# Logit weights of two token groups from one fp32 transpose, their products in fp32 on quarters of the array's columns

## The chip, the core and the metric

The kernel runs on one NeuronCore of one Trainium2 chip. The metric is the device time of one execution in microseconds; the median of three runs of the kernel before is 355.45 us (355.38 to 355.95). Engines are named as the profile names them: PE (TensorE's products; PEld its weight loads), DVE (VectorE), ACT (ScalarE), POOL (GpSimd), SP (SyncE, which issues the DMAs). PE's clock has two levels, 1.2 and 2.4 GHz; the profiled execution has a mean granted clock of 0.994, and 1.00 in every stretch that is read below.

## The reference, cut to what matters

```python
# attention: q, k, v are (2, 8, 576, 64); x becomes (1152, 512)
q_p, k_p = phi(q * scale), phi(k * scale)          # exp features, 128 of them
x = (q_p @ (k_p^T v)) / (q_p @ sum(k_p) + 1e-6)
# a dense layer, 512 -> 2048 -> 512
h = x @ w_in
g = h * (1 / (1 + exp(-1.702 * h)))
x2 = g @ w_out
# one expert per token
logits = x2 @ w_gate                                # (1152, 8)
expert_idx = argmax(logits, axis=1)
gate_w = softmax(logits)[expert_idx]
# tokens in order take the places of their expert until `capacity` (288) is full
out[i] = gate_w[i] * (relu(x2[i] @ w1[e]) @ w2[e])  # e = expert_idx[i]; 0 where no place was left
```

The dense layer's weights arrive as 64-bit floats and are decoded on the chip. w_in and w_out are cut along the 2048 into 16 chunks of 128 (m = 0 to 15).

## The kernel before

**Numbers.** Products that need fp32 accuracy are made of three fp32r products: a value is split into hi (rounded to fp32r) and lo (the rest), and mm3 (lines 81 to 84) adds hi*hi, hi*lo and lo*hi. Attention's own products and all transposes except those of w_out take plain fp32.

**Tokens.** The 1152 tokens form four groups G of GS = 288. Groups 0 and 2 go all the way: do_h makes h_ps for one chunk m (12 products of 128x288), gelu is taken twice by ACT (ghi in fp32r, line 544; g32 in fp32, line 545), DVE subtracts (glo, line 546), and do_y adds the chunk's share to four PSUM banks (12 more products). Of groups 1 and 3 only the logits are wanted at first; whether their tokens have a place left is found out later, and in these data no later branch runs. Their logits are taken without x2: with wp = w_out @ w_gate, a 2048 x 8 matrix, logits = g @ wp.

**Logit weights.** For each m, four steps on PE make 128 rows of wp: do_wt(m, 0) and do_wt(m, 1) transpose the chunk of w_out, hi and lo apart (four transposes each against identr, line 576; ACT copies each, line 577); do_wg multiplies them with w_gate (eight products of 128 columns, lines 585 and 587; ACT copies, line 589); do_wp transposes the 16x128 result back (line 594), and DVE reduces and splits it (lines 596 to 598). do_lg then adds g @ wp of one (G, m) to the bank lgt_ps with two products, ghi and glo (lines 610 and 613); groups 1 and 3 share the bank's 32 rows.

**Order.** The order of the work is a list of slots: seq has one do_h for each slot, by rounds. Round r has (0, r), (1, r - 3) and (3, r - 6) as far as they exist (L1 = 3, L3 = 6), 48 slots, then 16 slots of group 2. do_consume (do_y or do_lg) of a slot comes two slots later. slot(n, f) hangs other work on slot n: decoding, logit weights (do_wt at the slot of (1, m), the next steps half a slot apart), logits, choice of the experts, loads. A scheduler then places each engine's instructions, in about this order, and adds the waits; each engine runs its own list strictly in order.

**Decoding.** Each of the 32 chunks (in and out in turn) takes three DVE instructions, a, b and c (lines 220, 223, 226), through the int32 tile wf (two buffers) and back into every second word of the raw tile wraw; then d: ACT rounds hi (line 232) and POOL subtracts lo (line 233). Six chunks are decoded in the attention stage (P["dec"], steps 13 to 28), the other 26 from the dense layer's first slots on, 0.9 to 1 slot apart.

**Banks.** PSUM has eight banks: A (2: projections, h_ps), B and C (4: pj, then y), L and M. mbank alternates between L and M, and gives M alone while lgt_ps holds L.

Of the kernel before, what the change touches and what calls it, by code (L numbers as in the profile page):

```python
# [19 lines left out]
def linear_attention__moe__top1_moe_kernel(  # L20
# [106 lines left out]
    identr = const.tile([128, 128], F32R, name="identr")  # L127
    nc.vector.tensor_copy(identr, ident)
# [62 lines left out]
    w_raw = {}  # L191
# [19 lines left out]
    def decode(kind, m):  # L211
# [5 lines left out]
        f = gp.tile([128, DM], I32, tag="wf", name="wf", bufs=2)  # L217

# [240 lines left out]
    for s in range(NS + 1):  # L459
# [46 lines left out]
    wg_f = const.tile([128, KD, E], F32, name="wg_f")  # L506
    nc.sync.dma_start(out=wg_f, in_=moe2_w_gate.rearrange("(c p) e -> p c e", p=128))
    wg = const.tile([128, KD, 2, E], F32R, name="wg")
    nc.vector.tensor_copy(wg[:, :, 0], wg_f)
    nc.vector.tensor_tensor(wg[:, :, 1], wg_f, wg[:, :, 0].bitcast(F32), ALU.subtract)  # L510
# [7 lines left out]
    for r in range(NF + L3):  # L518
# [15 lines left out]
    def do_h(G, m):  # L534
# [32 lines left out]

    wts, wws = {}, {}

    def do_wt(m, i):  # L570
        src = w_out(m)[i]
        dst = gp.tile([128, DM], F32R, tag=f"wt{i}", name=f"wt{i}", bufs=1)
        ps = mbank("wt_ps")
        for c in range(KD):
            dc = slice(c * 128, c * 128 + 128)
            nc.tensor.transpose(ps[:, dc].bitcast(F32R), src[:, dc], identr)  # L576
        nc.scalar.copy(dst, ps)  # L577
        wts.setdefault(m, []).append(dst)

    def do_wg(m):  # L580
        th, tl = wts.pop(m)
        ps = mbank("wg_ps")
        for c in range(KD):
            dc = slice(c * 128, c * 128 + 128)
            nc.tensor.matmul(ps[:2 * E, :128], wg[:, c].rearrange("p a e -> p (a e)"), th[:, dc],
                             start=(c == 0), stop=False)
            nc.tensor.matmul(ps[:E, :128], wg[:, c, 0], tl[:, dc], start=False, stop=(c == KD - 1))
        t = gp.tile([2 * E, 128], F32, tag="wgt", name="wgt", bufs=1)
        nc.scalar.copy(t, ps[:2 * E, :128])
        wws[m] = t  # L590

    def do_wp(m):
        ps = mbank("wp_ps")
        nc.tensor.transpose(ps[:, :2 * E], wws.pop(m), ident[:2 * E, :2 * E])
        f = gp.tile([128, E], F32, tag="wpf", name="wpf", bufs=1)
        nc.vector.tensor_reduce(f, ps[:, :2 * E].rearrange("p (a e) -> p e a", a=2), AX, ALU.add)
        nc.vector.tensor_copy(wp[:, 2 * m + 1, 0], f)
        nc.vector.tensor_tensor(wp[:, 2 * m + 1, 1], f, wp[:, 2 * m + 1, 0].bitcast(F32), ALU.subtract)

    def do_lg(G, m):  # L600


        first = not held
        if first:
            held.append(bank("L", "lgt_ps"))
        g3 = G // 2
        ghi, glo = gs.pop((G, m))
        o = held[0]
        w = wp[:, 2 * m + 1 - g3:2 * m + 3 - g3].rearrange("p m a e -> p (m a e)")
        nc.tensor.matmul(o[:4 * E, :GS], w, ghi, start=first, stop=False)  # L610
# [3 lines left out]
        if last:  # L614
            nc.scalar.copy(lgt, held.pop()[:4 * E, :GS])
# [42 lines left out]
    def do_logits(G):  # L658
        if G % 2 == 0:
# [20 lines left out]
        nc.vector.tensor_reduce(  # L680
# [375 lines left out]
```

## Time and profile before

| | |
|---|---|
| median of three runs | 355.45 us (355.38 to 355.95) |
| the profiled execution | 356.26 us, of which its span (first to last instruction) is 354.4 us |
| PE busy | 332.9 us, 94% of the span, 2633 products |
| PEld busy | 318.0 us |
| DVE busy | 221.1 us |
| ACT busy | 189.2 us |
| POOL busy | 56.9 us |
| share of PE in the chain that ended last | 69%; DVE 13%, issue 6%, ACT 4%, DMA 4% |

In the profile a product's duration (0.30 us for 128x288) is longer than its time in the array, since products are pipelined and their ends are modelled. What a product costs PE is read from starts: the start of the next one less its own. Attention takes the first 100 us or so, the dense layer with its logits lasts until about 300 us, the experts' work follows; the stages overlap.

### The profile page before, as it was taken

The numbers are of one execution on the slowest core, as the hardware profiler recorded it, in microseconds if no ns is written. First come the engines' busy times: TensorE is split into PE (matmuls) and PEld (weight loads), VectorE is DVE, ScalarE is ACT, GpSimd is POOL, SyncE is SP. The second block draws the span as 40 slices with busy tenths as digits, with TensorE's granted clock in tenths as the row PEclk, the third lists the DMA queues.
The fourth block names the chain that finished last, engine by engine and source line by source line (L and its number), as shares of the span: only waits on it lengthen the run. The fifth ranks groups of instructions, "written<-read, shape, count | busy, mean of one in ns | idle before, by whom it ended". The sixth has DMA issues, their size and how long they took to land.

```text
span 354.4 us, 6927 instructions
## 1 busy us (share of the span) xinstructions
PE 332.9 (94%) x2633; PEld 318.0 (90%) x2633; DVE 221.1 (62%) x520; ACT 189.2 (53%) x485; POOL 56.9 (16%) x65
## 2 busy tenths in 40 slices
PE   5999999899979999999999999999999999999991
PEld 4899999788979999988889998999999999998990
DVE  6678889776799988999952224424552312758322
ACT  3798988789545655545544344444444222256312
POOL 3111202110124542455430000000000001010000
PEclk9999999999999999999999999999999999999997
DMA  6996632210034553555300000250330000184202
GB/s 178 294 339 171 199 123 82 98 60 2 2 118 128 173 157 108 165 167 179 118 2 1 2 2 1 67 172 2 118 120 0 2 0 2 38 278 164 67 0 75
DMA packets 29080, 35.20 MB, mean 99 GB/s; under 512 B 5360, under 2 KB 23792, under 8 KB 29040
## 3 DMA queue, kind: packets, MB, share of 16 engines
q1 hardware_dynamic: 29040, 34.69, 31.2%
q8 instruction: 22, 0.36, 0.4%
q14 instruction: 18, 0.15, 0.1%
HBM read 32.33 MB, written 2.36 MB: 98 GB/s over the span
## 4 chain that ended last, share of the span: by engine, by line
PE 69%; DVE 13%; issue 6%; ACT 4%; DMA 4%; SPq 2%; DVEq 0%; ACTq 0%
PE h_ps L82 10%; PE h_ps L84 9%; PE h_ps L83 9%; PE y L82 6%; PE y L83 6%; PE y L84 6%; PE nps L348 4%; PE kvp L323 4%; DVE wf L223 3%; DVE wraw L226 3%; DMA eraw<-in_moe_w_dram 2%; PE t L337 2%; DVE x_lo L383 2%; DVE glo L546 2%; PE wt_ps L576 2%
## 5 line engine op out<-in xcount | busy, mean ns | idle before, releaser
L544 ACT ACTIVATE ghi<-h_ps 128x288 fp32r<-128x288 f32 x64 | 26.3, 411 | 64.8 <-PE h_ps L84 64.8
L546 DVE TENSOR_TENSOR glo<-g,ghi 128x288 fp32r<-128x288 f32 x64 | 29.7, 465 | 39.9 <-ACT g L545 38.1
L220 DVE TENSOR_SCALAR wf<-wraw 128x512 int32<-128x512 int32 x32 | 35.1, 1098 | 0.3 <-DMA wraw<-in_moe_w_in_dram 0.3
L292 DVE TENSOR_REDUCE nb<-pj 128x4 f32<-128x512 f32 (+1 forms) x40 | 25.1, 632 | 4.5 <-PE pj L84 4.4
L794 DVE TENSOR_TENSOR el<-eraw,eh 128x1024 fp32r<-128x1024 f32 x16 | 19.5, 1223 | 12.7 <-ACT eh L793 12.7
L226 DVE SCALAR_TENSOR_TENSOR wraw<-wraw,wf 128x512 int32<-128x512 int32 x32 | 25.9, 809 | 0.2
L545 ACT ACTIVATE g<-h_ps 128x288 f32<-128x288 f32 x64 | 26.0, 406 | 0.0
L82 PE MATMUL pj<-om_hi,xh 128*128 128x256 f32 x72 | 23.9, 332 | 1.4 <-ACT qp L305 1.4
L793 ACT CAST eh<-eraw 128x1024 fp32r<-128x1024 f32 x16 | 16.7, 1048 | 13.9 <-issue 8.2
L864 POOL MEMSET base<- 96x1536 f32 x2 | 2.8, 1379 | 127.7 <-PE h_ps L84 127.7
L223 DVE SCALAR_TENSOR_TENSOR wf<-wraw,wf 128x512 int32<-128x512 int32 x32 | 22.5, 704 | 0.0
L305 ACT ACTIVATE qp<-pj,nb 128x128 f32<-128x128 f32 x72 | 21.7, 404 | 0.1
L305 ACT ACTIVATE kp<-pj,nb 128x128 f32<-128x128 f32 x72 | 21.4, 392 | 0.0
L83 PE MATMUL pj<-om_lo,xh 128*128 128x256 f32 x72 | 21.1, 293 | 0.0
L84 PE MATMUL pj<-om_hi,xl 128*128 128x256 f32 x72 | 21.0, 292 | 0.0
L82 PE MATMUL h_ps<-x_hi,win1h 128*128 128x288 f32 x64 | 20.1, 315 | 0.0
L269 ACT CAST xh<-tp 128x256 fp32r<-128x256 f32 (+1 forms) x40 | 14.7, 368 | 10.1 <-PE tp L266 10.0
L323 PE MATMUL kvp<-vt,kp 128*128 128x65 f32 (+1 forms) x144 | 20.0, 270 | 0.1
L82 PE MATMUL h_ps<-x_hi,win2h 128*128 128x288 f32 x64 | 19.9, 310 | 0.0
L82 PE MATMUL h_ps<-x_hi,win0h 128*128 128x288 f32 x64 | 19.8, 309 | 0.0
L577 ACT CAST wt<-wt_ps 128x512 fp32r<-128x512 f32 x32 | 19.0, 593 | 1.1 <-PE wt_ps L576 1.1
L82 PE MATMUL y<-hhi,eh 128*128 128x288 f32 x64 | 19.0, 297 | 0.6 <-DVE z L825 0.6
(229 smaller groups left out, 1147.3 us busy)
## 6 DMA issues: line engine op xcount, KB each, us to landing
wraw<-in_moe_w_in_dram SPq DMA_DIRECT2D x16, 512.0 KB, 3.6
wraw<-in_moe_w_out_dram SPq DMA_DIRECT2D x16, 512.0 KB, 3.5
eraw<-in_moe_w_dram SPq DMA_DIRECT2D x16, 512.0 KB, 4.8
qk_raw<-in_v_dram SPq DMA_DIRECT2D x4, 512.0 KB, 5.1
qk_raw<-in_q_dram SPq DMA_DIRECT2D x4, 512.0 KB, 5.2
qk_raw<-in_k_dram SPq DMA_DIRECT2D x3, 512.0 KB, 5.3
out_dram<-zer SPq DMA_DIRECT2D x2, 576.0 KB, 5.0
out_dram<-base SPq DMA_DIRECT2D x6, 192.0 KB, 2.3
```

Source lines behind the costliest of these rows:

```text
L82: nc.tensor.matmul(o, lh, rh, start=start, stop=False)
L83: nc.tensor.matmul(o, lh, rl, start=False, stop=False)
L84: nc.tensor.matmul(o, ll, rh, start=False, stop=stop)
L220: nc.vector.tensor_scalar(f, high, 3, 0x3FFFFFF8, ALU.logical_shift_left, ALU.bitwise_and)
L223: nc.vector.scalar_tensor_tensor(f, high, -0x40000000, f, ALU.bitwise_and, ALU.bitwise_or)
L226: nc.vector.scalar_tensor_tensor(low, low, 29, f, ALU.logical_shift_right, ALU.bitwise_or)
L292: mark["M", s] = nc.vector.tensor_reduce(nb[:, :nj], pj[:, :nj * M].rearrange("p (a m) -> p a m", m=M), AX, ALU.min)
L305: nc.scalar.activation(t[:, i], pj[:, i * M:(i + 1) * M], ACTF.Exp, bias=nb[:, i:i + 1], scale=-1.0)
L323: nc.tensor.matmul(ps[:, o:o + n], kp[:, i], vts[p][:, u, c0:c0 + n], start=(f == 0), stop=(f == NU - 1))
L544: nc.scalar.activation(ghi, ps[:, :GS], ACTF.Gelu_apprx_sigmoid)
L545: mark["a"] = nc.scalar.activation(g32, ps[:, :GS], ACTF.Gelu_apprx_sigmoid)
L546: mark["v"] = nc.vector.tensor_tensor(glo, g32, ghi.bitcast(F32), ALU.subtract)
```

## The change

- decode writes its last step into wf, not back into wraw, so wraw is free for the next load after step c, and wf (still two buffers) is held until ACT, POOL and, of an out chunk, PE have read it.
- do_wt makes one transpose in fp32 of the decoded chunk in wf (four PE transposes against ident, not two times four against identr), right behind the chunk's decoding. The first three out chunks are decoded in the attention stage, and their three steps (do_wt, do_wg, do_wp) are now there too, four, six and eight steps after their decoding begins.
- do_wg multiplies in fp32. Each of the four 128-deep pieces of w_gate (padded to 32 columns) goes to a quarter of the array's columns and a quarter of the bank's rows; do_wp adds the four quarters by one product with the 0/1 matrix fold8 and turns the result round.
- of groups 1 and 3 gelu is taken once, in fp32 (g1); no ghi, no glo. g1 and g32 share five buffers.
- do_lg keeps up to four (G, m) and run_lg then makes their products in fp32, one for each quarter of the columns: group 1 even m, group 1 odd m, group 3 even m, group 3 odd m. The quarters are added when the logits are read.
- L3 is 5, not 6: group 3 starts a round earlier.
- w_gate is loaded in the attention stage (step 12), and the two transposes before the logits of groups 1 and 3 take 64 and 128 rows instead of 32.

```diff
-P = dict(..., l1=3, l3=6, wt=0, wh=0.5, db=0.5, ...)
+P = dict(..., l1=3, l3=5, db=0.5, ...)
...
         f = gp.tile([128, DM], I32, tag="wf", name="wf", bufs=2)
+        if kind == "out":
+            wfs[m] = f
...
         def c():
-            nc.vector.scalar_tensor_tensor(low, low, 29, f, ALU.logical_shift_right, ALU.bitwise_or)
+            nc.vector.scalar_tensor_tensor(f, low, 29, f, ALU.logical_shift_right, ALU.bitwise_or)
 
         def d():
-            v = low.bitcast(F32)
+            v = f.bitcast(F32)
...
+    wg_f = const.tile([128, KD, 32], F32, name="wg_f")
+    wp = gate.tile([128, NF, 32], F32, name="wp")
+    fold8 = const.tile([128, E], F32, name="fold8")
...
+    def do_wt(m):
+        src = wfs.pop(m).bitcast(F32)
+        dst = gp.tile([128, DM], F32, tag="wt", name="wt", bufs=1)
+        ps = mbank("wt_ps")
+        for c in range(KD):
+            dc = slice(c * 128, c * 128 + 128)
+            nc.tensor.transpose(ps[:, dc], src[:, dc], ident)
+        nc.scalar.copy(dst, ps)
+        wts[m] = dst
+
+    def do_wg(m):
+        t = wts.pop(m)
+        ps = mbank("wg_ps")
+        for c in range(KD):
+            nc.tensor.matmul(ps[32 * c:32 * c + 32, :128], wg_f[:, c], t[:, c * 128:(c + 1) * 128],
+                             start=True, stop=True)
+        t = gp.tile([128, 128], F32, tag="wgt", name="wgt", bufs=1)
+        nc.scalar.copy(t, ps[:, :128])
+        wws[m] = t
+
+    def do_wp(m):
+        ps = mbank("wp_ps")
+        nc.tensor.matmul(ps[:, :E], wws.pop(m), fold8, start=True, stop=True)
+        nc.vector.tensor_copy(wp[:, m, 0:E], ps[:, :E])
...
             at(s + 4, load_next)
+            kd, m = wseq[wl[1] - 1]
+            if kd == "out":
+                at(s + 4, lambda m=m: do_wt(m))
+                at(s + 6, lambda m=m: do_wg(m))
+                at(s + 8, lambda m=m: do_wp(m))
...
-    def do_h(G, m):
+    def do_h(G, m, full=False):
...
+        if G % 2 and not full:
+            g1 = gp.tile([128, GS], F32, tag="g1", name="g1", bufs=5)
+            mark["a"] = nc.scalar.activation(g1, ps[:, :GS], ACTF.Gelu_apprx_sigmoid)
+            gs[G, m] = g1
+            return
...
     def do_lg(G, m):
-        first = not held
-        if first:
-            held.append(bank("L", "lgt_ps"))
-        g3 = G // 2
-        ghi, glo = gs.pop((G, m))
-        o = held[0]
-        w = wp[:, 2 * m + 1 - g3:2 * m + 3 - g3].rearrange("p m a e -> p (m a e)")
-        nc.tensor.matmul(o[:4 * E, :GS], w, ghi, start=first, stop=False)
-        n = E + 2 * E * g3
-        last = G == 3 and m == NF - 1
-        nc.tensor.matmul(o[:n, :GS], w[:, :n], glo, start=False, stop=last)
...
+        i = G - 1 + m % 2
+        if i in lgq:
+            run_lg()
+        lgq[i] = (m, gs.pop((G, m)))
+        if len(lgq) == 4 or (G, m) == (3, NF - 1):
+            run_lg()
...
+    def run_lg():
+        if not held:
+            held.append(bank("L", "lgt_ps"))
+        for i, (m, g) in sorted(lgq.items()):
+            nc.tensor.matmul(held[0][32 * i:32 * i + 32, :GS], wp[:, m], g, start=(m < 2), stop=(m >= NF - 2))
+        lgq.clear()
...
         slot(n + P["dd"], load_next)
+        kd, m = wseq[wl[1] - 1]
+        if kd == "out":
+            slot(n + P["dd"], lambda: do_wt(m))
+            slot(n + P["dd"] + 1, lambda: do_wg(m))
+            slot(n + P["dd"] + 2, lambda: do_wp(m))
...
-    for m in range(NF):
-        n = at_slot[1, m] + P["wt"]
-        h = P["wh"]
-        slot(n, lambda m=m: do_wt(m, 0))
-        slot(n + h, lambda m=m: do_wt(m, 1))
-        slot(n + 2 * h, lambda m=m: do_wg(m))
-        slot(n + 3 * h, lambda m=m: do_wp(m))
```

**PE in the middle of the dense layer, before.** The last product of a do_h, the two logit products of one (G, m), four transposes of w_out's hi half, and the next do_h (h_ps is its result, win the split weights, lgt_ps the logits' bank):

```order
L84 MATMUL h_ps<-x_hi,win1l 128x288
L610 MATMUL lgt_ps<-ghi,wp 32x288
L613 MATMUL lgt_ps<-glo,wp 24x288
L576 MATMUL wt_ps<-identr,wout1h 128x128 x4
L82 MATMUL h_ps<-x_hi,win0h 128x288
L83 MATMUL h_ps<-x_lo,win0h 128x288
```

The same engine and stage with the change (line numbers are those of the changed file; g is an fp32 gelu result, the number its tile):

```order
L84 MATMUL h_ps<-x_hi,win2l 128x288
L633 MATMUL lgt_ps<-g_2394,wp 32x288
L633 MATMUL lgt_ps<-g_2507,wp 32x288
L633 MATMUL lgt_ps<-g_2428,wp 32x288
L633 MATMUL lgt_ps<-g_2540,wp 32x288
L487 MATMUL wg_ps<-wt,wg_f 32x128 x4
L82 MATMUL h_ps<-x_hi,win1h 128x288
```

Two products for each (G, m), 64 in all, have become one for each, in seven runs of four and two runs of two; the runs stand every second round.

**DVE in the same stage, before.** Rows of the decoding (L220, L223, L226 are a, b, c; the number behind wf and wraw is the buffer's use), the wp steps and glo:

```order
L226 SCALAR_TENSOR_TENSOR wraw_2484<-wraw_2484,wf_2544 128x512 [waits DVE_49,Pool_49]
L596 TENSOR_REDUCE wpf_2636<-wp_ps_2634 128x8 [waits PE_49]
L597 CAST wp_1464<-wpf_2636 128x8 [waits DVE_49]
L598 TENSOR_TENSOR wp_1464<-wpf_2636,wp_1464 128x8 [waits DVE_49]
L546 TENSOR_TENSOR glo_2630<-g32_2628,ghi_2629 128x288 [waits Activation_49]
L223 SCALAR_TENSOR_TENSOR wf_2597<-wraw_2519,wf_2597 128x512
L220 TENSOR_SCALAR wf_2643<-wraw_2555 128x512 [waits DMAHW7_49]
L226 SCALAR_TENSOR_TENSOR wraw_2519<-wraw_2519,wf_2597 128x512 [waits DVE_49,Pool_49]
L546 TENSOR_TENSOR glo_2663<-g32_2661,ghi_2662 128x288 [waits PE_49,Activation_49]
```

And with the change:

```order
L220 TENSOR_SCALAR wf_2255<-wraw_2187 128x512 [waits DMAHW7_49,Pool_49]
L496 COPY wp_151<-wp_ps_2287 128x8 [waits PE_49]
L223 SCALAR_TENSOR_TENSOR wf_2255<-wraw_2187,wf_2255 128x512 [waits DVE_49]
L226 SCALAR_TENSOR_TENSOR wf_2255<-wraw_2187,wf_2255 128x512 [waits DVE_49]
L220 TENSOR_SCALAR wf_2285<-wraw_2225 128x512 [waits DMAHW0_49,PE_49,Pool_49]
L223 SCALAR_TENSOR_TENSOR wf_2285<-wraw_2225,wf_2285 128x512 [waits DVE_49]
L226 SCALAR_TENSOR_TENSOR wf_2285<-wraw_2225,wf_2285 128x512 [waits DVE_49]
L220 TENSOR_SCALAR wf_2330<-wraw_2266 128x512 [waits DMAHW1_49,Pool_49]
L496 COPY wp_151<-wp_ps_2366 128x8 [waits PE_49]
L593 TENSOR_TENSOR glo_2358<-g32_2360,ghi_2357 128x288 [waits Activation_49]
```

Step a (L220) now waits for POOL, and where the buffer held an out chunk also for PE, and stands ahead of b and c and of glo of group 0; there is one glo for three chunks where there was one for each.

## Rows read from the trace of the kernel before

**Rows 1.** Stretches: length, busy us (instructions) of each engine, PE's clock, DMA share, GB/s.

```profile
core 0: us, PE busy (x) PEld busy (x) DVE busy (x) ACT busy (x) POOL busy (x), PEclk, DMA share, GB/s
...
40.00:50.00 10.00, 9.78 (x88) 9.52 (x86) 8.73 (x24) 9.04 (x30) 1.31 (x1) 1.00 0.65 209
...
143.00:181.00 38.00, 35.41 (x282) 33.18 (x281) 37.62 (x60) 20.88 (x50) 18.37 (x12) 1.00 0.46 139
181.00:215.00 34.00, 33.48 (x272) 31.87 (x271) 9.16 (x29) 14.61 (x40) 1.31 (x1) 1.00 0.01 1
```

**Rows 2.** PE's waits over the whole span: us in total, times, longest.

```profile
PE lgt_ps L610 <- DVE wp L598: 3.1, 4, 0.9
```

**Rows 3.** Timeline of PE at two such waits: start us, duration us, instruction.

```profile
152.23 0.30 PE L84 MATMUL h_ps<-x_hi,win1l 128*128 128x288 f32 x1
153.38 0.32 PE L610 MATMUL lgt_ps<-ghi,wp 128*32 128x288 f32 x1 [0.85 <-DVE wp L598]
...
161.80 0.29 PE L84 MATMUL h_ps<-x_hi,win1l 128*128 128x288 f32 x1
```

**Rows 4.** Timeline of DVE: an early decoding step, then the stretch before the first wait.

```profile
91.30 0.42 DVE L220 TENSOR_SCALAR wf<-wraw 128x512 int32<-128x512 int32 x1
...
150.71 1.53 DVE L220 TENSOR_SCALAR wf<-wraw 128x512 int32<-128x512 int32 x1
152.16 0.68 DVE L226 SCALAR_TENSOR_TENSOR wraw<-wraw,wf 128x512 int32<-128x512 int32 x1
152.76 0.16 DVE L596 TENSOR_REDUCE wpf<-wp_ps 128x8 f32<-128x16 f32 x1
...
153.24 0.45 DVE L546 TENSOR_TENSOR glo<-g,ghi 128x288 fp32r<-128x288 f32 x1
```

**Rows 5.** Timeline of POOL in the same stretch.

```profile
150.59 1.36 POOL L233 TENSOR_TENSOR wout2l<-wraw,wout2h 128x512 fp32r<-128x512 f32 x1 [1.66 <-ACT wout2h L232]
```

**Rows 6.** Timeline of PE around each step of the logit weights and logits.

```profile
129.72 0.30 PE L84 MATMUL h_ps<-x_hi,win0l 128*128 128x288 f32 x1
129.86 0.46 PE L576 MATMUL wt_ps<-identr,wout0l 128*128 128x128 f32 x4
...
130.36 0.30 PE L83 MATMUL y<-glo,wout1h 128*128 128x288 f32 x1
...
131.82 0.22 PE L585 MATMUL wg_ps<-wt,wg 128*16 128x128 f32 x1
...
132.49 0.29 PE L83 MATMUL h_ps<-x_lo,win1h 128*128 128x288 f32 x1
...
133.82 0.29 PE L84 MATMUL h_ps<-x_hi,win1l 128*128 128x288 f32 x1
...
134.44 0.30 PE L83 MATMUL h_ps<-x_lo,win1h 128*128 128x288 f32 x1
...
135.11 0.29 PE L610 MATMUL lgt_ps<-ghi,wp 128*32 128x288 f32 x1
...
135.37 0.29 PE L82 MATMUL h_ps<-x_hi,win1h 128*128 128x288 f32 x1
```

**Rows 7.** Timeline of PE in attention: fp32 products and transposes in a row.

```profile
40.38 0.61 PE L352 MATMUL nps<-kvs,qt 128*128 128x130 f32 x4
40.82 0.60 PE L390 MATMUL xps<-ident,xr 128*128 128x128 f32 x4
41.26 1.00 PE L323 MATMUL kvp<-vt,kp 128*128 128x65 f32 x8
42.10 0.39 PE L266 MATMUL tp<-ident,qk_raw 128*128 128x128 f32 x2
```

**Rows 8.** Groups of PE by line and shape: count, busy us, mean ns.

```profile
L352 PE MATMUL nps<-kvs,qt 128*128 128x130 f32 x16 | 2.6, 287 | 0.4 <-DVE x_lo L383 0.4
```

**Rows 9.** Groups of ACT by line and shape: the copies of a transposed chunk.

```profile
L577 ACT CAST wt<-wt_ps 128x512 fp32r<-128x512 f32 x32 | 19.0, 593 | 1.1 <-PE wt_ps L576 1.1
```

**Rows 10.** Instructions of two lines: ns min/median/max, first and last start us.

```profile
L774 SPq DMA_DIRECT2D eraw<-in_moe_w_dram x8: 372/373/525, 227.3 to 309.7; - x8
...
L793 ACT CAST eh<-eraw x16: 1039/1048/1052, 246.1 to 324.6; 128x1024 fp32r<-128x1024 f32 x16
```

More of the change, by code (lines that the diff above doesn't have):

```diff
@@ L190, in linear_attention__moe__top1_moe_kernel @@
     w_pair(w0p, "out", 0)
-    w_raw = {}
+    w_raw, wfs = {}, {}
     def load_w(kind, m):
@@ L450, in paced, with load_gate @@
         return g
+    wg_f = const.tile([128, KD, 32], F32, name="wg_f")
+    wg = const.tile([128, KD, 2, E], F32R, name="wg")
+    wp = gate.tile([128, NF, 32], F32, name="wp")
+    fold8 = const.tile([128, E], F32, name="fold8")
+    for t in (wg_f, wp):
+        nc.gpsimd.memset(t, 0.0)
+    nc.gpsimd.tensor_tensor(fold8, ident[:, 0:E], ident[:, 32:32 + E], ALU.add)
+    for i in (64, 96):
+        nc.gpsimd.tensor_tensor(fold8, fold8, ident[:, i:i + E], ALU.add)
+    def load_gate():
+        nc.sync.dma_start(out=wg_f[:, :, 0:E], in_=moe2_w_gate.rearrange("(c p) e -> p c e", p=128))
+        nc.vector.tensor_copy(wg[:, :, 0], wg_f[:, :, 0:E])
+        nc.vector.tensor_tensor(wg[:, :, 1], wg_f[:, :, 0:E], wg[:, :, 0].bitcast(F32), ALU.subtract)
+    wts, wws = {}, {}
+    def do_wt(m):
[20 more added lines that the diff above has]
+        nc.vector.tensor_copy(wp[:, m, 0:E], ps[:, :E])
     out_t = out.rearrange("(a p) d -> p a d", p=TT)
@@ L472, in linear_attention__moe__top1_moe_kernel @@
             load_next(4)
+            load_gate()
         if s in DEC_AT:
@@ L505, in linear_attention__moe__top1_moe_kernel @@
     giota = const_iota("giota", TT, [NG], [[1, NG]], 0, 0)
[L506 to L510, printed above, removed]
     L1, L3 = P["l1"], P["l3"]
@@ L544, in do_h @@
         nc.scalar.activation(ghi, ps[:, :GS], ACTF.Gelu_apprx_sigmoid)
+        g32 = gp.tile([128, GS], F32, tag="g1", name="g32", bufs=5)
         mark["a"] = nc.scalar.activation(g32, ps[:, :GS], ACTF.Gelu_apprx_sigmoid)
@@ L565, in do_y @@
                 nc.vector.tensor_tensor(x_lo[sl], y, x_hi[sl].bitcast(F32), ALU.subtract)
[L568 to L598, printed above, removed]
-    def do_lg(G, m):
-        first = not held
-        if first:
-            held.append(bank("L", "lgt_ps"))
-        g3 = G // 2
-        ghi, glo = gs.pop((G, m))
-        o = held[0]
-        w = wp[:, 2 * m + 1 - g3:2 * m + 3 - g3].rearrange("p m a e -> p (m a e)")
-        nc.tensor.matmul(o[:4 * E, :GS], w, ghi, start=first, stop=False)
-        n = E + 2 * E * g3
-        last = G == 3 and m == NF - 1
-        nc.tensor.matmul(o[:n, :GS], w[:, :n], glo, start=False, stop=last)
-        if last:
-            nc.scalar.copy(lgt, held.pop()[:4 * E, :GS])
+    def do_lg(G, m):
+        i = G - 1 + m % 2
[4 more added lines that the diff above has]
+            run_lg()
+        if (G, m) == (3, NF - 1):
+            held_t.append(gp.tile([128, GS], F32, tag="g1", name="lgt", bufs=5))
+            nc.scalar.copy(held_t[0], held.pop()[:, :GS])
@@ L666, in do_logits @@
                                  start=False, stop=(c == KD - 1))
-            t = gp.tile([2 * E, GS], F32, tag="g32", name="lgy", bufs=2)
+            t = gp.tile([2 * E, GS], F32, tag="g1", name="lgy", bufs=5)
             nc.scalar.copy(t, ps[:2 * E, :GS])
@@ L670, in do_logits @@
         else:
-            n = 4 * E
-            t = lgt
+            n = 64 if G == 1 else 128
+            t = held_t[0]
         ps = mbank("lgr_ps")
@@ L988, in linear_attention__moe__top1_moe_kernel @@
                     if m < NF:
-                        do_h(3, m)
+                        do_h(3, m, True)
                     if m:
```

18 lines of the change are left out of this document (5 added, 13 removed).

## The prediction

> **What bounds the kernel now.** I read the busy time by stretches first [rows 1]. In attention (40 to 50 us) PE is busy 9.78 of 10 us, with ACT at 9.04 close behind it; in the dense layer at 35.41 of 38 and 33.48 of 34 us, at the granted clock of 1.00, the upper of its two levels (2.4 GHz). So what is added to or taken from PE's list moves the end, wherever PE does not wait. From 143 to 181 us, while chunks are decoded, DVE is busier than PE: 37.62 of 38 us against 35.41. After 181 us, with the decoding done, DVE falls to 9.16 of 34 us and PE is alone at the limit.
>
> The second view is PE's waits. Of the product of group 1's logits PE waits four times for wp, which comes from DVE, 3.1 us in all [rows 2]. The timeline of PE shows such a wait: the product before it starts at 152.23, the logit product at 153.38, so 1.15 us from start to start where 0.13 is usual [rows 3]. The listed waits begin at the modelled end of the product before (0.30 after its start), so each hides some 0.17 us; the four cost 3.1 + 4 x 0.17 = 3.8 us.
>
> The third is DVE's own timeline there [rows 4]. Step a of a decoding takes 0.42 us at 91.30, and 1.53 us at 150.71, where POOL began its subtraction 0.12 us earlier and took 1.36 us [rows 5]: beside POOL, a lasts until POOL is done. A round holds three chunks, so 3 x (1.46 + 0.60 + 0.60 + 0.37) us for a, b, c and glo (c's 0.60 is 152.16 to 152.76; b has c's form; glo in its usual pitch) plus 0.48 us for the three wp steps (152.76 to 153.24) = 9.57 us; and PE's round is 161.80 - 152.23 = 9.57 us [rows 3]. In these four rounds DVE sets the pace, in all others PE.
>
> **The change part by part.** The sum is made against the profiled execution's 356.26 us, which is 0.8 us above the median of the runs.
>
> *What goes on PE.* A 128x288 product costs 0.13 us (L610 at 135.11 to L82 at 135.37 is two of them) [rows 6]. From starts, less the 0.13 us products in between: four transposes of a half chunk 0.64 - 0.26 = 0.38 us (129.72 to 130.36), 32 times: 12.2; do_wg 0.67 - 0.13 = 0.54 us (131.82 to 132.49), 16 times: 8.6; do_wp 0.62 - 0.26 = 0.36 us (133.82 to 134.44), 16 times: 5.8; the logits 0.26 us for each (G, m), 32 times: 8.3. Together 34.9 us.
>
> *What comes on PE.* (1) Transposes of 128 columns in fp32 follow each other every 0.11 us (L390, four in 0.44 us) [rows 7]; with the 0.08 us by which the product behind four transposes is late before as after, 16 x 0.52 = 8.3 us. (2) An fp32 product stands in the trace as two records: line 352 has eight products in the program and 16 records [rows 8]. A record costs 0.11 us with 130 columns, and about as much with 65 (L352, 0.44 us for four; L323, 0.84 us for eight) [rows 7]. do_wp is then 2 x 0.11 us and a late product behind it, 16 x 0.29 = 4.6 us. (3) No row shows products on different quarters of the columns next to each other, so do_wg and the logits are bounded from both sides. A record of do_wg (128 columns) is 0.11 us. A record of the logits has 288 columns: 0.11 x 288 / 130 = 0.244 us, at the least the 0.13 us of an fp32r product of that size. do_wg has 4 products, eight records. If nothing overlaps, they take eight lengths; if all quarters run side by side, two. Between them: PE takes its list in order, and the second record of a product needs the same quarter as the first, so it can only start when that one is through; the first record of the next product can run beside it. That makes five lengths for four products and three for two. I take this value, since the starts in the trace follow the program's list throughout [rows 7]. Then do_wg costs 16 x (5 x 0.11 + 0.05 late) = 9.6 us (4.3 to 14.9), and the logits, in seven runs of four and two of two, 41 x 0.244 = 10.0 us (2.3 to 15.6). Together 32.5 us, so PE's list is 2.4 us shorter: 13.3 with full overlap, 8.5 longer with none.
>
> *The waits for wp.* wp is now made right after the decoding, many slots before its use, and DVE loses two of three glo and two of three wp steps: a round needs 3 x (0.36 + 1.2) + 0.6 = 5.3 us if a never meets POOL and 3 x (1.46 + 1.2) + 0.6 = 8.6 us if it always does. PE's round with three decodings is 48 x 0.13 + 1.5 x (0.52 + 0.60 + 0.29) + 0.6 = 9.0 us. DVE stays below it; the 3.8 us go, and PE's own list is late next.
>
> *New waits on wf.* Step a waits for POOL's subtraction two chunks earlier, and for PE's transposes where that chunk was an out chunk; b, c and glo of group 0 queue behind it, and do_y two slots later waits for glo. Two slots are 6 us of PE, against at most 0.45 for glo, 1.53 for a and 1.2 for b and c: nothing, as long as DVE's round is shorter than PE's. If not, see the second rival below.
>
> *Attention.* The first three sets of logit weights move into a stage where PE is as full as in the dense layer, so their PE time counts as above. ACT gets three copies of a chunk (0.59 us each) [rows 9] and three smaller ones, 2 to 3 us on an engine that is busy 9 of 10; and nine more uses go through the banks L and M, which attention's transposes and copies need in turn. Between 0, if PE's added work covers ACT's, and 4 us if ACT's time and some bank waits come on top. I take 1.5, nearer the lower end, as PE is the fuller of the two.
>
> *Small things.* Six transposes before the logits of groups 1 and 3 have 64 or 128 rows, not 32: at most six of 0.11 us, on PE; I take 0.4. A gelu less and its subtraction free ACT (32 x 0.41 us or so) and DVE, which is nothing after 181 us. Group 0's logits come a slot later through L3; the first expert's loads are issued at 227.3 and first used at 246.1 [rows 10], which covers one slot of 3 us. w_gate's load goes in behind four weight loads and is needed steps later; the earlier release of wraw starts loads sooner, and DVE doesn't wait for them.
>
> *Sum.* -2.4 - 3.8 + 1.5 + 0.4 = -4.3 us: 352.0 us for a profiled execution, 351.2 us for the median. The bounds of the unshown costs alone give 336 to 365 us.
>
> **The rivals.** *Full overlap on the quarters* (two lengths for four products): 21.6 us on PE in place of 34.9. -13.3 - 3.8 + 1.9 = -15.2, and up to 3 us back in six rounds of decoding, where PE's round would be 8.1 us and DVE's up to 8.6: about 341.5. For it: nothing in the trace forbids it; against it: two records for each product, and starts in order. The Trainium skill ("TensorE: Matmul & The Clock Gate", Part 3, Packing small matmuls) has matmuls on different column tiles start a few ns apart and measured 2.38 times for three of them; it also has matmuls start and end in program order, which is the five lengths if the two records share a tile. No run here shows either yet.
>
> *No overlap* (eight lengths): +8.5 - 3.8 + 1.9 = +6.6, a time of 362. Slower than before as soon as four products need more than about six lengths (each further length is 9 x 0.244 + 16 x 0.11 = 4.0 us in all). For it: every neighbouring pair of the trace runs one behind the other.
>
> *The two wf buffers lock PE to DVE.* If a regularly meets POOL and waits for PE's transposes, c comes late, PE stands at the next do_wt as it now stands at the logits (0.9 us each [rows 2]), in half of the 13 sets of the dense layer: +6, a time of 357. It decides once DVE's round exceeds PE's 9.0 us; 8.6 is its upper bound without new waits.
>
> *The overlap happens, but what PE saves is taken back elsewhere* (attention's ACT and banks at their upper end, a few waits on wf): 355.
>
> **How the numbers follow.** The forecast has 0.45, full overlap 0.22, none 0.17, the lock 0.11, the balance 0.05. The likeliest case is 351.2 us, by itself 347 to 355. A range that leaves out the far halves of full and of no overlap is 341 to 361. A measurement of this kernel can tell about 0.2%, or 0.7 us, from no change. Faster by more: 0.22 and most of 0.45, together 0.64; within: 0.07; slower: 0.29.
>
> **What would show it.** In PE's timeline the eight records of four products: pairs that start together with 0.24 us between pairs (five lengths), all within half a us (full), or evenly 0.24 apart (none). The waits for wp from DVE should be gone, DVE in the decoding stretch well under PE, and after it PE's round near 48 x 0.13 + 0.6 = 6.9 us against 6.2 + 2 x 0.38 + 0.54 + 0.36 + 0.52 = 8.4 us now. In attention PE's busy share should stay and the stage end some 4 to 6 us later. I'd be wrong if PE waits at do_wt for DVE, if attention grows by much more than its added PE time, or if a record of 288 columns is not 0.24 us.

## The result, and the profile after

The changed kernel takes 352.0 us in the median (350.5 to 353.9), beside 355.7 for the kernel before on the same chip: a ratio of 0.989, 95% interval 0.986 to 0.992. That is 3.7 us faster; 351.2 was forecast. The profiled execution took 352.38 us (356.26 before), its span is 350.2 us (354.4 before). That the total came out right is luck: two of its terms were wrong by 6 to 9 us each, with opposite signs.

The stretches that answer to [rows 1], with the same columns:

```profile
143.00:181.00 38.00, 32.29 (x262) 28.80 (x252) 27.84 (x42) 15.33 (x35) 15.85 (x12) 0.96 0.45 140
181.00:215.00 34.00, 33.86 (x274) 31.41 (x272) 7.36 (x15) 10.40 (x26) 5.51 (x4) 1.00 0.00 1
```

While chunks are decoded, DVE is no longer full (27.84 of 38 us, 37.62 before), but PE is less busy too: 32.29 against 35.41. Nobody is at the limit there, so the engines wait for each other. PE's waits that answer to [rows 2] (us in total, times, longest) say where; the waits for wp at the logits are gone:

```profile
PE wt_ps L478 <- DVE wp L496: 5.7, 5, 2.5
...
PE wt_ps L478 <- DVE wf L226: 0.7, 2, 0.4
```

Line 478 is the transposes of do_wt, line 496 DVE's copy of the 128x8 product wp_ps into wp. The transposes don't read wp. They need bank M, which is the only one for wt_ps, wg_ps and wp_ps as long as the logits hold L, and which is free only when wp_ps has been copied. The longest such wait, on PE (start us, duration us, instruction, idle time before):

```profile
146.95 0.29 PE L84 MATMUL h_ps<-x_hi,win2l 128*128 128x288 f32 x1
149.75 1.11 PE L478 MATMUL wt_ps<-ident,wf 128*128 128x128 f32 x4 [2.51 <-DVE wp L496]
...
151.86 0.44 PE L84 MATMUL h_ps<-x_hi,win2l 128*128 128x288 f32 x1
152.10 0.44 PE L82 MATMUL h_ps<-x_hi,win2h 128*128 128x288 f32 x1
```

And on DVE and POOL at the same time:

```profile
144.87 1.75 POOL L233 TENSOR_TENSOR win2l<-wf,win2h 128x512 fp32r<-128x512 f32 x1 [1.79 <-ACT win2h L232]
146.58 1.30 POOL L233 TENSOR_TENSOR wout2l<-wf,wout2h 128x512 fp32r<-128x512 f32 x1
...
146.66 1.51 DVE L220 TENSOR_SCALAR wf<-wraw 128x512 int32<-128x512 int32 x1 [1.20 <-POOL win2l L233]
148.20 0.69 DVE L223 SCALAR_TENSOR_TENSOR wf<-wraw,wf 128x512 int32<-128x512 int32 x1
148.93 0.69 DVE L226 SCALAR_TENSOR_TENSOR wf<-wraw,wf 128x512 int32<-128x512 int32 x1
149.54 0.16 DVE L496 COPY wp<-wp_ps 128x8 f32<-128x8 f32 x1
```

Read it backwards. The copy takes 0.16 us, and its product had been on PE since 146.46. But it stands in DVE's queue behind steps a, b and c of a later chunk, and a (line 220) waited 1.20 us until POOL had done its subtraction, then took 1.51 us beside POOL's next one (0.42 alone [rows 4]). From starts, PE lost 149.75 - 146.95 - 0.13 = 2.67 us here.

There is a second price. Two stretches of PE's clock (columns as in [rows 1]):

```profile
147.00:149.70 2.70, 0.24 (x2) 0.00 (x1) 2.62 (x4) 0.00 (x0) 0.88 (x1) 0.99 0.65 209
149.80:153.00 3.20, 3.20 (x17) 2.92 (x20) 0.43 (x1) 0.59 (x1) 0.00 (x0) 0.50 0.51 164
```

PE did almost nothing for 2.7 us; in the 3.2 us behind that the granted clock is 0.50, the lower level (1.2 GHz), and products start 0.24 us apart (151.86 to 152.10) where 0.13 is usual. Nine products, the transposes and a do_wg at that pace cost some 1.4 us more: from the start of the transposes to that of the second product behind do_wg it is 3.82 us (149.75 to 153.57), where the same steps take 0.63 + 7 x 0.133 + 0.82 = 2.38 us at the upper clock.

The steps on the quarters, on the other hand, cost PE less than forecast. PE's timeline around do_wg, do_wp, a run of four logit products, and four undisturbed transposes:

```profile
159.39 0.29 PE L84 MATMUL y<-ghi,wout2l 128*128 128x288 f32 x1
159.61 0.43 PE L487 MATMUL wg_ps<-wt,wg_f 128*32 128x128 f32 x8
159.97 0.40 PE L82 MATMUL h_ps<-x_hi,win2h 128*128 128x288 f32 x1
160.21 0.29 PE L83 MATMUL h_ps<-x_lo,win2h 128*128 128x288 f32 x1
...
161.53 0.29 PE L84 MATMUL h_ps<-x_hi,win2l 128*128 128x288 f32 x1
161.66 0.28 PE L495 MATMUL wp_ps<-fold,wgt 128*128 128x8 f32 x2
...
162.01 0.29 PE L83 MATMUL h_ps<-x_lo,win1h 128*128 128x288 f32 x1
...
189.26 0.30 PE L84 MATMUL h_ps<-x_hi,win3l 128*128 128x288 f32 x1
189.40 0.60 PE L478 MATMUL wt_ps<-ident,wf 128*128 128x128 f32 x4
...
189.97 0.30 PE L83 MATMUL h_ps<-x_lo,win3h 128*128 128x288 f32 x1
...
199.66 0.29 PE L84 MATMUL h_ps<-x_hi,win2l 128*128 128x288 f32 x1
199.89 0.69 PE L633 MATMUL lgt_ps<-g,wp 128*32 128x288 f32 x8
200.51 0.40 PE L82 MATMUL h_ps<-x_hi,win2h 128*128 128x288 f32 x1
200.75 0.30 PE L83 MATMUL h_ps<-x_lo,win2h 128*128 128x288 f32 x1
```

What a step costs PE: from the start of the product ahead of it to the start of the second product behind it, less two usual 0.133 us. The second one, because the first is late. So do_wg costs 0.82 - 0.27 = 0.55 us, do_wp 0.22, the transposes 0.45, a run of four logit products 1.09 - 0.27 = 0.82 us, or 0.48 where it stands directly ahead of a do_wg. The run of four in three slices (length; PE and PEld busy, records under way in brackets), of line 633 alone:

```profile
199.88:200.02 0.14, 0.13 (x4) 0.14 (x8) 1.00 0.00 0
200.02:200.14 0.12, 0.12 (x4) 0.02 (x4) 1.00 0.00 0
200.14:200.20 0.06, 0.06 (x8) 0.00 (x0) 1.00 0.00 0
```

Eight records belong to the four products. Four are under way at once, and then the other four. Their starts are 0, 7, 13, 20 and 267, 273, 280, 287 ns: side by side, one length behind the other.

### The profile page after: what moved, and what is told of

Its sections match the earlier page's. It is cut to its first block, busy times and chain, and to the rows that moved or that the text cites. A ratio compares the mean times of both kernels' runs of the same rounds, so it can differ in the third digit from the quotient of the medians.

```text
span 350.2 us, 6676 instructions
## 1 busy us (share of the span) xinstructions
PE 326.3 (93%) x2585; PEld 307.3 (88%) x2585; DVE 191.2 (55%) x454; ACT 171.3 (49%) x437; POOL 59.0 (17%) x70
## 4 chain that ended last, share of the span: by engine, by line
PE 42%; DVE 3%; DMA 2%; issue 2%; ACT 1%; DVEq 0%; ACTq 0%
PE h_ps L82 8%; PE h_ps L83 8%; PE h_ps L84 8%; PE y L82 5%; PE y L83 5%; PE y L84 5%; DMA eraw<-in_moe_w_dram 2%; PE lgt_ps L633 1%; DVE el L812 1%; PE zt_ps L848 1%; ACT eh L811 1%; DVE wf L223 1%; PE wt_ps L478 0%; DVE base L889 0%; DVE wf L220 0%
## 5 line engine op out<-in xcount | busy, mean ns | idle before, releaser
L593 DVE TENSOR_TENSOR glo<-g,ghi 128x288 fp32r<-128x288 f32 x32 | 16.7, 522 | 55.7 <-ACT g L592 55.4
L590 ACT ACTIVATE ghi<-h_ps 128x288 fp32r<-128x288 f32 x32 | 13.1, 410 | 40.3 <-PE h_ps L84 40.2
L585 ACT ACTIVATE g<-h_ps 128x288 f32<-128x288 f32 x32 | 13.2, 412 | 33.1 <-PE h_ps L84 28.1
L226 DVE SCALAR_TENSOR_TENSOR wf<-wraw,wf 128x512 int32<-128x512 int32 x32 | 27.9, 871 | 0.6
L220 DVE TENSOR_SCALAR wf<-wraw 128x512 int32<-128x512 int32 x32 | 18.1, 566 | 15.1 <-POOL wout1l L233 4.3
L223 DVE SCALAR_TENSOR_TENSOR wf<-wraw,wf 128x512 int32<-128x512 int32 x32 | 22.8, 716 | 0.2
L83 PE MATMUL pj<-om_lo,xh 128*128 128x256 f32 x72 | 21.6, 300 | 0.0
L323 PE MATMUL kvp<-vt,kp 128*128 128x65 f32 (+1 forms) x144 | 20.9, 272 | 0.0
L84 PE MATMUL h_ps<-x_hi,win0l 128*128 128x288 f32 x64 | 19.4, 303 | 0.0
L83 PE MATMUL h_ps<-x_lo,win2h 128*128 128x288 f32 x64 | 19.4, 303 | 0.0
```

The source lines that it names most:

```text
L83: nc.tensor.matmul(o, lh, rl, start=False, stop=False)
L84: nc.tensor.matmul(o, ll, rh, start=False, stop=stop)
L220: nc.vector.tensor_scalar(f, high, 3, 0x3FFFFFF8, ALU.logical_shift_left, ALU.bitwise_and)
L223: nc.vector.scalar_tensor_tensor(f, high, -0x40000000, f, ALU.bitwise_and, ALU.bitwise_or)
L226: nc.vector.scalar_tensor_tensor(f, low, 29, f, ALU.logical_shift_right, ALU.bitwise_or)
L323: nc.tensor.matmul(ps[:, o:o + n], kp[:, i], vts[p][:, u, c0:c0 + n], start=(f == 0), stop=(f == NU - 1))
```

## Experiments

Two questions had to be settled: what the four quarters are worth, and what took the gain back. Each kernel was timed beside the kernel before (356.1 to 356.4 us in these series); the ratios are to that kernel, with 95% intervals. The first four started from two theories of the waits: A, the copy of wp holds the bank from within DVE's queue; B, the forecast's own rival, the two wf buffers lock PE to DVE.

**The copy of wp on ScalarE.**

```diff
-        nc.vector.tensor_copy(wp[:, m, 0:E], ps[:, :E])
+        (nc.vector.tensor_copy if m < 3 else nc.scalar.copy)(wp[:, m, 0:E], ps[:, :E])
```

> The copy of wp out of its bank goes from VectorE to ScalarE for the chunks m >= 3 (those of the dense layer); nothing else is changed. Theory A (bank M: PE's transposes at line 478 wait because the bank still holds wp_ps, whose copy stands in VectorE's queue behind a decoding step that waits for POOL): the waits at line 478, 7.5 us above the undisturbed 0.46 us a set, go, and with them the stretches at the lower clock: 352 - 8 = 343 to 345 us, under 1 us of waits at line 478. Theory B (the forecast's lock: the two wf buffers; VectorE's decoding sets the round): PE then waits at the same place for step c (line 226) instead of the copy, the time stays within 350 to 352 us.

Measured: 347.7 us, 0.976 (0.973 to 0.978). The waits for the copy are gone, 4.3 us of time with them, and the clock stays at 1.00 in 143 to 181 us. It is half of what A expected. What is left is a wait for step c, which B had named as its sign, though with another time (350 to 352 us):

```profile
PE wt_ps L478 <- DVE wf L226: 2.0, 4, 0.7
```

Here DVE runs almost without gaps (35.76 of 38 us busy), and its timeline, with POOL's row below, shows why a chunk takes it 2.78 us (153.03 to 155.81):

```profile
153.03 0.41 DVE L220 TENSOR_SCALAR wf<-wraw 128x512 int32<-128x512 int32 x1
153.48 0.69 DVE L223 SCALAR_TENSOR_TENSOR wf<-wraw,wf 128x512 int32<-128x512 int32 x1
154.21 1.68 DVE L226 SCALAR_TENSOR_TENSOR wf<-wraw,wf 128x512 int32<-128x512 int32 x1
155.81 0.41 DVE L220 TENSOR_SCALAR wf<-wraw 128x512 int32<-128x512 int32 x1
...
153.84 1.50 POOL L233 TENSOR_TENSOR wout2l<-wf,wout2h 128x512 fp32r<-128x512 f32 x1 [1.28 <-ACT wout2h L232]
```

POOL works from 153.84 to 155.34; step c ends at 155.89, 0.55 us after POOL, though it takes 0.69 when alone (148.93 above). So c all but stood until POOL was done. It is no single case: in the changed kernel all 12 of the 96 decoding steps that began while POOL's subtraction was under way are lengthened (b and c to 1.67 us, each with its end 0.55 us behind POOL's), and none of the other 84. The Trainium skill ("SBUF — State Buffer", "Who interferes with whom") has VectorE's instructions with two SBUF inputs contend with GpSimd for a pair of ports that is an exclusive lock: who issues second is blocked, not slowed. These rows agree but for 0.14 us (0.55 instead of 0.69 behind POOL's end).

**Three buffers of wf**, with two of ghi and glo to make room; the copy stays on VectorE.

```diff
-        f = gp.tile([128, DM], I32, tag="wf", name="wf", bufs=2)
+        f = gp.tile([128, DM], I32, tag="wf", name="wf", bufs=3)
```

> The copy of wp stays on VectorE; wf has three buffers instead of two, and ghi and glo two instead of three to make the room. Theory A: step a no longer waits for POOL (1.2 us at 145.46 and at other places), but the copy still stands behind steps a, b and c, so the waits at line 478 shrink from 7.5 us to 3 to 5: 347 to 350 us. Theory B (the buffers are the lock): the waits go altogether, 343 to 345 us.

Measured: 354.2 us, 0.994 (0.991 to 0.996), no faster than the changed kernel (0.989). The waits are as before, and ScalarE's copy of the transposes is added to them:

```profile
PE wt_ps L478 <- DVE wp L496: 5.5, 4, 2.2
...
PE wg_ps L487 <- ACT wt L479: 1.8, 2, 0.9
```

Both numbers of the expectation failed. B is out: with a third buffer the waits for the copy stay (5.5 us against 5.7). What the two buffers of ghi and glo cost by themselves was not measured. A's number fell too, and that is a hint at the root: step a no longer stands for POOL, but now step c is stretched beside it (1.75 us at 147.99, POOL's subtraction from 147.86 for 1.33), and the copy comes at 149.66, as late as before.

**Both.**

> Both: the copy of wp on ScalarE for m >= 3, and three buffers of wf (ghi and glo two). Theory A: as with the copy alone, 342 to 345 us, within 1 us of it. Theory B: as with three buffers alone.

Measured: 348.1 us, 0.977 (0.975 to 0.980): the third buffer, with two of ghi and glo, adds nothing to the copy on ScalarE.

**Two quarters in place of four** (from the kernel with both): the logits of one group share a quarter.

```diff
-            nc.tensor.matmul(held[0][32 * i:32 * i + 32, :GS], wp[:, m], g, start=(m < 2), stop=(m >= NF - 2))
+            nc.tensor.matmul(held[0][32 * (i // 2):32 * (i // 2) + 32, :GS], wp[:, m], g, start=(m == 0), stop=(m == NF - 1))
```

> As the kernel with both, but the logits of group 1 all go to the first quarter of the columns and those of group 3 all to the second, so that of a run of four products two and two share a quarter; number and size of the products are the same. Theory A (records on different quarters run side by side, those on one quarter one after the other, 0.266 us each): a run of four takes 1.06 us in place of 0.53, a run of two the same: 9 x 0.53 = 4.8 us more than the kernel with both, and the starts in the trace at 0, 0.27, 0.53, 0.80 us. Rival C (the quarters have no part in it; what shortens the fp32 products is their 32 columns): no more than 0.5 us difference, starts as before.

Measured: 351.9 us, 0.988 (0.985 to 0.991), 3.8 us more than with four quarters (A had 4.8; by the starts below, 9 x 0.48 = 4.3). PE's timeline at a run of four, and at the first run, which has two products:

```profile
132.10 1.16 PE L633 MATMUL lgt_ps<-g,wp 128*32 128x288 f32 x4
133.19 0.39 PE L495 MATMUL wp_ps<-fold,wgt 128*128 128x8 f32 x2
...
195.78 1.17 PE L633 MATMUL lgt_ps<-g,wp 128*32 128x288 f32 x8
196.88 0.40 PE L82 MATMUL h_ps<-x_hi,win2h 128*128 128x288 f32 x1
```

A run of four takes 1.10 us to the next product where it took 0.62 (199.89 to 200.51); its records start at 0, 14, 267, 280, 510, 523, 752 and 765 ns. The run of two takes 1.09 us on one quarter (0, 267, 510, 752 ns) and 0.61 on two. So records on one quarter follow each other every 0.24 to 0.27 us, and those of different quarters run side by side: A's rule, and the forecast's 0.244 us a record. C is out. The same runs refute the order that the forecast took. On one quarter the two records of a product follow each other; on two quarters the records start at 0, 6, 266 and 273 ns. So the second product's first record does not wait for the first product's second record. Where a do_wg stands behind a run in this kernel, its products even pass the run, on the two quarters that the logits leave free:

```profile
161.57 0.93 PE L633 MATMUL lgt_ps<-g,wp 128*32 128x288 f32 x6
162.10 0.41 PE L487 MATMUL wg_ps<-wt,wg_f 128*32 128x128 f32 x4
162.32 0.42 PE L633 MATMUL lgt_ps<-g,wp 128*32 128x288 f32 x2
162.56 0.40 PE L487 MATMUL wg_ps<-wt,wg_f 128*32 128x128 f32 x4
```

The Trainium skill ("TensorE: Matmul & The Clock Gate", Part 3, "The mechanism") has matmuls start and end strictly in program order; for fp32 products of two records on different column quarters these starts differ from the order in which the kernel lists its products (the order in which their records were issued stands in no row).

**Transposes half a slot later** (from the copy on ScalarE).

```diff
-            slot(n + P["dd"], lambda: do_wt(m))
+            slot(n + P["dd"] + 0.5, lambda: do_wt(m))
```

> The kernel with the copy of wp on ScalarE (347.7 us), and do_wt of the dense layer hung half a slot later, so that it is no longer directly behind do_wp of the chunk before and step c of its chunk has more time. Theory A (what is left of waits at line 478 there, 2.5 us behind do_h and 1.0 us behind do_wp, is a matter of where PE meets the chunk): both go, 344 to 345.5 us. Rival B2 (VectorE's decoding, 35.8 of 38 us busy in that stretch, sets the round, and the waits come back at another place): 347 to 348 us.

Measured: 348.6 us, 0.978 (0.975 to 0.980), B2's number or a little over. The waits at line 478 go, and as long ones come at do_wg:

```profile
PE wg_ps L487 <- ACT wt L479: 2.2, 2, 1.1
```

So the waits have moved and not gone, as B2 said: it is not a matter of where PE meets the chunk. That the decoding sets the round is not shown by this run alone, since DVE is busy 33.05 of 38 us in it; the moves of POOL's subtraction below show it.

**The gelu split put back as load** (on the changed kernel; ScalarE's second gelu and VectorE's subtraction are made for groups 1 and 3 too, and not used).

```diff
+            ghi = gp.tile([128, GS], F32R, tag="ghi", name="ghi")
+            glo = gp.tile([128, GS], F32R, tag="glo", name="glo")
+            nc.scalar.activation(ghi, ps[:, :GS], ACTF.Gelu_apprx_sigmoid)
             mark["a"] = nc.scalar.activation(g1, ps[:, :GS], ACTF.Gelu_apprx_sigmoid)
+            nc.vector.tensor_tensor(glo, g1, ghi.bitcast(F32), ALU.subtract)
```

> The changed kernel with one part of the change undone in cost alone: of groups 1 and 3 ScalarE takes the second gelu again and VectorE subtracts (ghi and glo are made and not used); all products stay as they are. Theory A (after the change VectorE's queue in the decoding stretch is what PE waits for, through the bank that wp_ps holds): two more subtractions of 0.46 us a round stand before the copies, so waits at line 478 grow by 0.5 to 1 us a round: 354 to 357 us. Rival D (with PE's list as the limit, what VectorE and ScalarE do for groups 1 and 3 is hidden): 351.5 to 352.5 us.

Measured: 356.9 us, 1.003 (1.000 to 1.005): 4.9 us over the changed kernel, all of its gain. In the profiled execution (358.9 us, one of the three slowest of twelve) `wt_ps L478 <- DVE wp L496` grows to 6.8 us, do_wg waits 1.8 us for ScalarE's copy, and the clock of 143 to 181 us falls to 0.91. D is out. So with POOL's subtraction in the way, the gain of this change hangs on leaving out the second gelu, which is no work of PE; how it is without that subtraction was not run.

**do_wg and do_wp for two chunks at a time** (from the copy on ScalarE), ghi and glo with two buffers.

```diff
+        for i in range(2):
+            for c in range(KD):
+                nc.tensor.matmul(ps[32 * c:32 * c + 32, i * 128:i * 128 + 128], wg_f[:, c],
+                                 t[:, i, c * 128:(c + 1) * 128], start=True, stop=True)
```

> The kernel with the copy of wp on ScalarE (347.7 us), and do_wg and do_wp made for two chunks at a time (eight products on the quarters in a row, then two of line 495's; ghi and glo have two buffers to make the room). Theory E (a run on the quarters has a fixed price of about 0.31 us beside its records, paid once a run: a set of do_wg costs 0.55 us where its records last 0.24): eight runs fewer save 8 x 0.31 = 2.5 us, and do_wp up to 0.8: 344.5 to 345.5 us. Rival F (the price belongs to each product): a run of eight costs 1.1 us and the time stays within 347.2 to 348.2 us.

Measured: 346.7 us, 0.972 (0.969 to 0.974). A run of eight:

```profile
147.32 0.29 PE L84 MATMUL h_ps<-x_hi,win2l 128*128 128x288 f32 x1
147.54 0.64 PE L489 MATMUL wg_ps<-wt,wg_f 128*32 128x128 f32 x16
...
148.36 0.29 PE L83 MATMUL h_ps<-x_lo,win1h 128*128 128x288 f32 x1
```

It costs 1.04 - 0.27 = 0.77 us, where two runs of four cost 1.11. Four more products cost 0.22 us, so a run of its own costs some 0.33 us beside its records, and E holds on PE. The logits' runs agree: 0.82 us less two lengths of 0.245 is 0.33. The price goes with the quarters and not with fp32: four fp32 transposes on the whole array, between the same products, cost 0.455 us, with 0.11 us from record to record. The Trainium skill ("TensorEngine Tiling (Array Packing)", "Key Properties") says that a change of the tiling mode drains the engine; the fixed price agrees, and the page gives no number for it. Of the 2.5 us expected only 1.0 came through, while the waits for step c grew from 2.0 to 3.4 us.

**More buffers for the experts' split results** (from the pairs; hhi and hlo of even m take the five buffers of g1).

> The kernel of the pairs (346.7 us), with the experts' split results spread over more buffers, so that the wait of 1.9 us at 'h_ps <- DVE hlo' that two buffers brought there goes. Theory E (fixed price of a run on the quarters; the pairs really saved 2.8 to 3.1 us of PE, and 1.9 of it was lost at hlo): 344.5 to 345 us. Rival (the pairs' saving is lost to waits for VectorE's step c at the transposes, 3.4 us there against 2.0 before): 346.5 us.

Measured: 346.7 us, 0.970 (0.965 to 0.975), the rival's number. The wait at hlo stood in the profiled execution of the pairs, the slowest of seven (348.2 us); the other six (346.4 to 347.0) are as fast as this kernel, so it was probably not in them, though no profile shows that.

**The subtraction of the decoding on VectorE, not on POOL**, in the dense layer (from the copy on ScalarE).

```diff
-            nc.gpsimd.tensor_tensor(lo, v, hi.bitcast(F32), ALU.subtract)
+            lo_on[0].tensor_tensor(lo, v, hi.bitcast(F32), ALU.subtract)
...
+    lo_on[0] = nc.vector
     stA.close()
```

> The kernel with the copy of wp on ScalarE (347.7 us), and in the dense layer the subtraction of line 233 (lo of a decoded chunk) on VectorE instead of POOL. Theory G (VectorE is slow in decoding because POOL works beside it: step c takes 1.68 us there and 0.69 alone): c takes 0.7 us, the subtraction about 0.7 us, a chunk 2.5 us of VectorE in place of 2.8, no waits for POOL, and PE's 2.0 us of waits for step c go in part: 345.5 to 347 us. Rival H (VectorE has as much more to do as it gains, and waits for ScalarE's rounding in its own queue): 348 to 351 us.

Measured: 342.7 us, 0.959 (0.954 to 0.964), 5.0 us less, more than G expected. No wait at the transposes is left, and PE is busy 38.00 of 38 us in the stretch of 143 to 181 us.

**All of it.**

> Pairs, more buffers for the experts' split results, wp copied by ScalarE and the subtraction on VectorE together. If theories E and G hold: 342 to 344 us. If G falls: as the kernel with the pairs and buffers, or 1 to 3 us more.

Measured: 340.5 us, 0.954 (0.948 to 0.959), the fastest version. With nothing else at the limit the pairs are worth 2.2 us.

**The subtraction alone moved, on the changed kernel and on the kernel before.** Two runs with the same edit as above and nothing else.

> The changed kernel with one edit: in the dense layer the subtraction of line 233 is VectorE's instead of POOL's; the copy of wp stays on VectorE. Theory G (POOL's subtraction is the root: VectorE's queue stands at step a for it and runs slower beside it, and the copy that frees the bank stands in that queue): the 8.5 us lost at line 478 go nearly all, 343 to 345 us. Rival A alone (the copy's place in VectorE's queue is the cause, whatever stands ahead of it): 347 to 350 us.

> The kernel before with the same one edit. Theory G: the four rounds that VectorE set (3.8 us of waits for wp in all) become PE's, 351.5 to 353 us, and the change is then worth 8 to 9 us, as PE's shorter list says. Rival: VectorE, at 37.6 of 38 us there, only gets more to do (0.7 us a chunk): 356 to 360 us.

Measured: 342.5 us, 0.960 (0.956 to 0.965), for the changed kernel, and 351.6 us, 0.986 (0.981 to 0.990), for the kernel before. Both in the stretch of [rows 1], the changed kernel first:

```profile
143.00:181.00 38.00, 38.00 (x332) 35.11 (x330) 30.47 (x62) 19.63 (x44) 0.00 (x0) 1.00 0.44 137
...
143.00:181.00 38.00, 38.00 (x310) 36.52 (x308) 33.64 (x74) 22.78 (x54) 0.00 (x0) 1.00 0.44 135
```

And a chunk on DVE, in the changed kernel with the edit:

```profile
152.30 0.42 DVE L221 TENSOR_SCALAR wf<-wraw 128x512 int32<-128x512 int32 x1
152.76 0.69 DVE L224 SCALAR_TENSOR_TENSOR wf<-wraw,wf 128x512 int32<-128x512 int32 x1
153.37 0.69 DVE L234 TENSOR_TENSOR win2l<-wf,win2h 128x512 fp32r<-128x512 f32 x1
153.97 0.69 DVE L227 SCALAR_TENSOR_TENSOR wf<-wraw,wf 128x512 int32<-128x512 int32 x1
154.57 0.43 DVE L221 TENSOR_SCALAR wf<-wraw 128x512 int32<-128x512 int32 x1
```

A chunk takes 2.27 us of DVE (152.30 to 154.57) with the subtraction, and 2.78 without it beside POOL. In both kernels PE is then busy all of the 38 us, and no wait at the transposes or the logits is left. The copy of wp is still on VectorE here, and it makes no difference whether it is (342.5 and 342.7): its place in the queue does harm only when something ahead of it stands still. So POOL's subtraction is the root of what was lost, and the bank is one way by which it reached PE: with the copy on ScalarE 4.3 of the 9.5 us came back, and the rest stayed as long as POOL's subtraction did. G holds in both kernels. Between these two, where PE waits for DVE's decoding in neither, the change is worth 351.6 - 342.5 = 9.1 us.

## Why the forecast was right in its total and wrong in its terms

**What goes (34.9 us).** Held. By starts the steps of before cost 0.37, 0.56, 0.355 us and, undisturbed, 0.26 for a pair of logit products; 0.38, 0.54, 0.36 and 0.26 had been taken.

**What comes (32.5 us): mis-sized by 6.5.** Measured 16 x 0.455 for the transposes (7.3; forecast 8.3), 16 x 0.555 for do_wg (8.9; 9.6), 16 x 0.22 for do_wp (3.5; 4.6), and 6.3 for the logits (4 x 0.82 + 3 x 0.48 + 2 x 0.80; forecast 10.0): 26.0 us. The step that failed is "PE takes its list in order ... five lengths". Two lengths it is, the rival with 0.22. But the rival's 21.6 us was 4.4 off the other way, since neither had the fixed 0.33 us for each run on the quarters. For do_wg the two errors nearly cancel: 0.55 against 0.60 forecast, out of two lengths and the fixed price. PE's list became 34.9 - 26.0 = 8.9 us shorter, not 2.4; the 9.1 us between the last two runs are this number to within 0.4, with attention (below).

**The waits for wp (-3.8).** Held; they are gone, and moving POOL's subtraction in the kernel before takes 4.8 us, so they are most of what DVE cost there.

**New waits on wf ("nothing"): mis-sized by some 9.** At line 478 PE waits, over the 0.455 us of a set, some 8.5 us in all by starts, with 0.5 us of transposes at the lower clock in it, and that clock costs some 0.9 us more behind them. Three steps of the argument failed. It had wf's buffers as the only new resource, while the resource was bank M, which I had counted in attention alone: DVE's copy holds it, and do_wt needs it in the dense layer. It compared DVE's 8.6 us at most with PE's 9.0, but PE's round became 8.45 us (in the changed kernel with the subtraction on VectorE, where nothing stands in its way, two rounds go from 155.2 to 172.1), and DVE's beside POOL is three times 2.78 and glo, 8.8. And it took a queue at its sum of work, though PE, ACT, DVE and POOL wait for each other in turn there: a round of the changed kernel takes 10.1 us (155.2 to 175.4 is two), more than the list of any engine. The forecast named the sign ("wrong if PE waits at do_wt for DVE") and a price of 6 us for the lock, at 0.11. The overlap of the full-overlap rival and a wait at the place of the lock rival, by another resource, together make the result; as I had them, each was a case by itself, and that their errors cancelled in the total is luck.

**Attention (+1.5): mis-sized by some 1.3.** The first do_h starts 5.0 us later (86.4 against 81.4), of which 3 x 1.22 are the three sets. But the other 1.3 us are nearly all work that changed places: before, nine products of attention's projections (pj, 81.57 to 83.79, 1.2 us of PE by starts) stand behind the first do_h; with the change they stand ahead of it. So some 0.2 us were added. PE is busy 9.80 of 10 us in 40 to 50 us, as before.

**Small things (+0.4).** Nothing to be seen: the transposes before the logits cost 1.7 us in all, 1.8 before.

**Sum as measured.** By the runs: the change without the conflict -9.1 (PE's list -8.9, attention +0.2, the rest not traced); what DVE and POOL cost before, gone, -4.8 (356.4 to 351.6); what they cost after, 352.0 - 342.5 = +9.5. Together -4.4, against -3.7 measured directly; the 0.7 between is the difference of the kernel before from series to series (355.7 and 356.4).

**What would show it.** After the decoding PE's round is 6.8 us (199.89 to 213.48 is two), 6.9 forecast. Waits for wp gone: yes. DVE "well under PE": yes, but for the wrong reason, since it stood waiting.

## What to carry to other kernels

When a change makes the bounding engine's list shorter, work out the round of the next engine against the new round, not the old, and go through every PSUM bank in it: whose instruction frees it, and what stands ahead of that instruction in its queue. Work that POOL takes off VectorE is no relief when it blocks VectorE for longer than VectorE would need for it: here 1.0 us a chunk against 0.6. Small products on quarters of the array should stand in long runs: each run cost 0.33 us here beside its products, more than four fp32 products of 128 columns (0.22).

## What the runs showed of the hardware that I had not expected

The two records of an fp32 product on one quarter run one after the other (0.27 and 0.24 us at 288 columns), but records of other quarters pass them: four products on four quarters start 7 ns apart, and their second records likewise 0.267 us later. After a wait of 2.51 us on PE (until 149.75) the granted clock was 0.50 for 3.2 us, while after one of 2.17 us (until 171.47) it stayed at 1.00. And VectorE's decoding step of 0.69 us took 1.67 us or so whenever it began during POOL's two-input subtraction, which takes 1.27 to 1.30 us by itself.
